# Top-k attention and two MLPs: the softmax division moved from each head to each tile of tokens, with a new order

## The chip, the cores and the metric

One core of a Trainium2 chip runs the whole program. It has a matrix engine (TensorE, PE in the rows), a vector engine (VectorE, DVE), a scalar engine (ScalarE, ACT), GpSimd (POOL), and a sync engine (SP) whose queue issues the DMAs here. The metric is device microseconds (us) of one execution, the median of several.

## The reference

```python
scores = q @ k.T / 8                                   # 4 batches x 8 heads, 576 x 576, head size 64
kth    = the 32nd largest of each row
attn   = softmax(where(scores >= kth, scores, -1e9))
x      = (attn @ v), heads side by side: 2304 tokens x 512
h      = x @ w_in;  x = (h * sigmoid(1.702 h)) @ w_out           # 512 -> 2048 -> 512
h      = x @ w_in2; out = (P(h) / (Q(h) + 1e-6)) @ w_out2        # P cubic, Q = 1 + |b0||h| + |b1|h^2
```

## The kernel before

The 2304 tokens are 18 tiles of 128 rows. Attention runs as 144 steps, one for a tile and a head (tile-major, so eight steps make a tile). A step (`attend`) multiplies q and k on TensorE into a PSUM tile `S`; four rounds of `max` on VectorE, with `match_replace` between them, find the 32nd largest value of each row (tiles `mx`, `E`); ScalarE and GpSimd turn the scores into the numerators of the softmax (`nm`, `E`), split them into a high and a low f16 half (`A`), and a transposing DMA brings them to `AT`. Then `attend_av` makes the second product on TensorE, 15 matmuls into a PSUM slot `misc`, 64 columns of it the head's output and one more the sum of the numerators, because `V` has a column of ones.

Before the change VectorE takes the reciprocal of that sum (`r`, L704), and ScalarE copies the 64 columns from PSUM into the tile's row buffer `x` with `r` as its scale (L705). When a tile's eight heads are there, `x_done` rescales `x` where a group of tiles spans two batches (L756, 6 tiles of 18), makes the f16 high half on ScalarE (L757) and the low half on GpSimd (L758), and a transposing DMA writes `xh` (L760), the input of the first MLP.

The MLPs run in units over groups of two tiles (one in the last two groups): `u_h` (first product, L815), `u_act` (L835 and on), `u_o` (second product, L896 for the first MLP, L893 for the second). The weights of both are prepared on the chip at the start (`w_load`: a conversion on VectorE, L418 and L421, squares and sums on ScalarE, small matmuls L323).

Nobody writes the order of instructions by hand. Each operation is recorded with an engine, a duration, what it reads and writes, and a due time; some name a second engine (`alt`). `Program.schedule` then picks, again and again, the operation that can start first, and among several the one with the smallest due time plus an entry of the table `OFF` (by kind, engine and phase). All engines take their instructions in the order that comes out of this, so an instruction that waits holds up all behind it on its engine. The due times follow from constants such as `LAV` (how many steps the second product lags), `UW` (steps for a unit), `W1P` and `W2P` (when the weights are prepared).

Of the kernel before, what the change touches and what calls it, by code (L numbers as in the profile page):

```python
# [7 lines left out]
F32 = mybir.dt.float32  # L8
# [3 lines left out]
AF = mybir.ActivationFunctionType  # L12
# [209 lines left out]
def kernel(  # L222
# [461 lines left out]
    def attend_av(i, prio):  # L684
# [62 lines left out]
    def x_done(t, prio):  # L747
# [314 lines left out]
LAV = 2.171  # L1062
# [11 lines left out]
KLAG = 7.3553  # L1074
QLAG = 3.6483
NKH = 1
NQH = 1
W1P = -0.5495
W2P = 6.1579
W1R = 0.6406  # L1080
W2R = 0.8231
LATE = 2
MLAG = 3.9112
SWITCH = 59.94
OLAG = 1.2959
UW = 1.2171
ALATE = -329.15
OFF = {
    ('attend', 'ACT'): 4.75,
    ('attend', 'ACT', 0): 0.44,  # L1090
    ('attend', 'ACT', 1): -0.72,
    ('attend', 'ACT', 2): 0.58,
    ('attend', 'ACT', 3): 46.78,
    ('attend', 'ALT'): 22.03,
    ('attend', 'DVE'): 39.57,
    ('attend', 'DVE', 0): 20.59,
    ('attend', 'DVE', 1): -3.17,
    ('attend', 'DVE', 2): -6.61,
    ('attend', 'DVE', 3): 0.24,
    ('attend', 'PE'): -148.65,  # L1100
    ('attend', 'PE', 0): -18.34,
    ('attend', 'PE', 1): 2.41,
    ('attend', 'PE', 2): -17.08,
    ('attend', 'PE', 3): 5.2,
    ('attend', 'POOL'): -5.3,
    ('attend', 'POOL', 0): -19.7,
    ('attend', 'POOL', 1): -32.31,
    ('attend', 'POOL', 2): 7.63,
    ('attend', 'POOL', 3): 3.96,
    ('attend', 'SP'): -25.93,  # L1110
    ('attend', 'SP', 0): -10.33,
    ('attend', 'SP', 1): -14.06,
    ('attend', 'SP', 2): -2.97,
    ('attend', 'SP', 3): 15.67,
    ('attend_av', 'ACT'): -139.96,
    ('attend_av', 'ACT', 0): -44.41,
    ('attend_av', 'ACT', 1): -1.02,
    ('attend_av', 'ACT', 2): 7.97,
    ('attend_av', 'ACT', 3): 6.06,
    ('attend_av', 'ALT'): 2.68,  # L1120
    ('attend_av', 'DVE'): -8.3,
    ('attend_av', 'DVE', 0): 4.69,
    ('attend_av', 'DVE', 1): -6.19,
    ('attend_av', 'DVE', 2): -3.12,
    ('attend_av', 'DVE', 3): 0.88,
    ('attend_av', 'PE'): -70.15,
    ('attend_av', 'PE', 1): 5.75,
    ('attend_av', 'PE', 2): 14.49,
    ('k_prep', 'ACT'): -1.49,
    ('k_prep', 'ACT', 0): 0.39,  # L1130
    ('k_prep', 'ACT', 1): -7.7,
    ('k_prep', 'ACT', 2): 41.38,
    ('k_prep', 'ACT', 3): -6.15,
    ('k_prep', 'ALT'): 7.45,
    ('k_prep', 'DVE'): 27.22,
    ('k_prep', 'DVE', 0): 9.09,
    ('k_prep', 'DVE', 1): -9.7,
    ('k_prep', 'DVE', 2): 51.8,
    ('k_prep', 'DVE', 3): -32.69,
    ('k_prep', 'PE'): 24.7,  # L1140
# [290 lines left out]
```

## Time and profile before

| | us |
|---|---|
| median of 3 runs (1252.35 to 1254.08) | 1253.32 |
| the profiled execution, its own time | 1253.18 |
| its span, from the first to the last instruction | 1251.4 |
| TensorE matmuls busy | 1047.7 (84%) |
| VectorE busy | 1078.1 (86%) |
| ScalarE busy | 1048.0 (84%) |
| GpSimd busy | 773.6 (62%) |

The profiled execution lies 0.14 us under the median, and 1.8 us of its time are outside the span. Busy times overlap, and each is a mean over stages with different limits; a group's busy time counts overlapped stretches of one engine only once, so instructions that follow each other closely add less than their own duration.

### The profile page before, as it was taken

To read this page: it belongs to the slowest core of one execution; us is meant where nothing else is said; L and a number is where in the kernel's file an instruction comes from. 1 tells how busy PE (TensorE), PEld (TensorE's weight loads), DVE (VectorE), ACT (ScalarE), POOL (GpSimd) and SP (SyncE) were. 2 spreads that over 40 slices of the span, in tenths; PEclk is the share of its full clock that TensorE was granted. 3 is DMA by queue.
4 is the path that set the end of the run, shared out by engine and by line. 5 is a ranking of instruction groups with operands and counts; after the bars stand their busy time and mean duration, and the time that the engine had idled before them with its cause. 6 is when DMAs were issued, how large, how long until landed. Compare 5 with 4: busy or idle time off the path is not lost.

```text
span 1251.4 us, 26010 instructions
## 1 busy us (share of the span) xinstructions
PE 1047.7 (84%) x9196; PEld 712.6 (57%) x9196; DVE 1078.1 (86%) x2423; ACT 1048.0 (84%) x1931; POOL 773.6 (62%) x1095
## 2 busy tenths in 40 slices
PE   0223464659899999999999999999999999999998
PEld 0122342537556766676567666756666677676664
DVE  6899999999999999999999999989999997424243
ACT  7989887878989999999998988788888988666675
POOL 6888888876767678766785685467657653211110
PEclk9999995778999999999999999999999999999999
DMA  9847999967889568967697579557856854634375
GB/s 317 251 113 205 204 272 278 266 143 176 174 208 230 92 133 208 220 130 158 154 217 146 113 193 206 116 135 178 188 102 132 214 123 96 194 102 161 118 260 186
DMA packets 366146, 222.44 MB, mean 178 GB/s; under 512 B 316608, under 2 KB 328896, under 8 KB 366016
## 3 DMA queue, kind: packets, MB, share of 16 engines
q1 hardware_dynamic: 366016, 220.78, 71.6%
q8 instruction: 72, 1.18, 0.4%
q14 instruction: 58, 0.48, 0.1%
HBM read 136.32 MB, written 13.11 MB: 119 GB/s over the span
## 4 chain that ended last, share of the span: by engine, by line
PE 37%; DVE 30%; ACT 11%; POOL 8%; DMA 8%; issue 5%; SPq 1%; POOLq 0%; DVEq 0%; ACTq 0%
PE h L815 16%; DVE mx L663 11%; DVE E L665 10%; PE acc L893 9%; PE acc L896 7%; DMA AT<-A 4%; ACT t L835 3%; PE misc L694 3%; PE S L655 2%; POOL A L675 2%; POOL t L839 2%; DVE t L843 1%; DMA ring<-in_moe_w_out_dram 1%; DVE t L848 1%; DVE t L840 1%
## 5 line engine op out<-in xcount | busy, mean ns | idle before, releaser
L663 DVE MAX8 mx<-E 128x8 f32<-128x576 f32 x432 | 319.5, 750 | 2.6
L893 PE MATMUL acc<-ring,t 128*128 128x512 f32 x576 | 270.3, 603 | 7.4 <-DVE t L840 5.3
L675 POOL TENSOR_TENSOR A<-E,A 128x576 f16<-128x576 f32 x144 | 188.4, 1310 | 63.8 <-ACT A L673 58.3
L815 PE MATMUL h<-xh,W 128*128 128x128 f16 (+1 forms) x2688 | 214.1, 240 | 10.8 <-DVE t L848 9.5
L815 PEld LDWEIGHTS <-W 128*128 128x128 f16 x2688 | 193.3, 101 | 38.9 <-issue 14.6
L665 DVE MATCH_REPLACE8 E<-mx,E 128x576 f32<-128x576 f32 x288 | 213.4, 742 | 0.0
L815 PE MATMUL h<-yh,ring 128*128 128x256 f16 (+1 forms) x1920 | 208.8, 263 | 4.3 <-ACT t L835 3.6
L815 PEld LDWEIGHTS <-ring 128*128 128x128 f16 x1920 | 170.6, 98 | 51.6 <-issue 29.5
L839 POOL TENSOR_TENSOR t<-t,t 128x512 f32<-128x512 f32 x114 | 151.9, 1333 | 44.9 <-ACT t L835 35.0
L896 PE MATMUL acc<-W,gh 128*128 128x512 f16 x576 | 173.7, 383 | 0.1
L893 PEld LDWEIGHTS acc<-ring,t 128*128 128x128 f32 x576 | 102.0, 191 | 102.7 <-issue 84.0
L872 POOL TENSOR_TENSOR gl<-t,gh 128x512 f16<-128x512 f32 x72 | 84.4, 1172 | 118.9 <-ACT gh L870 117.7
L655 PE MATMUL S<-K,qs 128*128 128x288 f16 (+1 forms) x640 | 113.8, 308 | 49.9 <-ACT E L668 47.2
L671 ACT ACTIVATE E<-E,nm,ei 128x576 f32<-128x576 f32 x144 | 124.4, 865 | 17.2 <-POOL nm L670 15.9
L835 ACT ACTIVATE t<-h,cf 128x512 f32<-128x512 f32 (+1 forms) x160 | 94.2, 641 | 42.7 <-PE h L815 40.5
L694 PE MATMUL misc<-V,AT 128*128 128x65 f16 (+5 forms) x2400 | 102.9, 200 | 31.6 <-DMA AT<-A 24.5
L694 PEld LDWEIGHTS <-AT 128*128 128x128 f16 (+2 forms) x2400 | 94.1, 104 | 58.9 <-DMA AT<-A 39.0
L668 ACT ACTIVATE E<-S,mx 128x576 f32<-128x576 f32 x144 | 105.7, 736 | 16.8 <-DVE mx L663 10.5
L655 PEld LDWEIGHTS <-qs 128*128 128x128 f16 (+1 forms) x640 | 65.2, 106 | 91.1 <-issue 70.4
L663 DVE MAX8 mx<-S 128x8 f32<-128x576 f32 x144 | 108.3, 754 | 5.2 <-PE S L655 4.2
L896 PE MATMUL acc<-W,gl 128*128 128x512 f16 x288 | 110.2, 382 | 1.9 <-POOL gl L872 1.8
L835 ACT ACTIVATE t<-h,cf,cf 128x512 f32<-128x512 f32 (+1 forms) x160 | 110.5, 745 | 0.0
(161 smaller groups left out, 1807.0 us busy)
## 6 DMA issues: line engine op xcount, KB each, us to landing
ring<-scr SPq DMA_DIRECT2D x160, 512.0 KB, 4.5
ring<-in_moe_w_out_dram SPq DMA_DIRECT2D x12, 1024.0 KB, 7.5
ring<-in_moe_w_in_dram SPq DMA_DIRECT2D x9, 1024.0 KB, 6.8
ld<-in_v_dram SPq DMA_DIRECT2D x32, 256.0 KB, 3.8
out_dram<-t SPq DMA_DIRECT2D x18, 256.0 KB, 4.2
ld<-in_k_dram SPq DMA_DIRECT2D x16, 256.0 KB, 4.2
lq<-in_q_dram SPq DMA_DIRECT2D x32, 128.0 KB, 3.4
yh<-in_moe_w_in_dram SPq DMA_DIRECT2D x4, 1024.0 KB, 8.4
```

The costliest lines, as they stand in the source:

```text
L655: PE.matmul(s[:n, c, :SH], qs[:, 2 * (h % 4) + x, :n], K[:, h % 2, c * SH:(c + 1) * SH], start=(x == 0), stop=(x == 1))
L663: op("DVE", dve(S, not r), lambda r=r: DVE.max(mx[:, r], w.t if r else sv()), [w if r else s], [mx], prio)
L665: op("DVE", dve(S, not r) + 0.068, lambda r=r: DVE.match_replace(w.t if r else two(w.t), mx[:, r], w.t if r else sv(), NEG), [mx, w if r e ...
L668: op("ACT", act(S, True) + APA, lambda: ACT.activation(two(e.t), sv(), AF.Prelu, bias=mx[:, 3, 7:8], scale=-1.0, alpha=NEAR), [s, mx], [e] ...
L671: op("ACT", act(S) + 0.2, lambda: ACT.activation(e.t, e.t, AF.Exp, bias=nm.t, scale=es()), [e, nm, ei], [e], prio)
L675: lo = lambda en: en.tensor_tensor(A[:, 1, :S], e.t, A[:, 0, :S], ALU.subtract)
L694: PE.matmul(ps[r0:r0 + n, :hi - lo], at[:kp, x, j, r0:r0 + n], V[:kp, h % 2, j, lo:hi], start=(j == 0 and lo == D and x == 0), stop=(j == ...
L815: PE.matmul(o, w[:, half, kd * 256 + jj * P: kd * 256 + (jj + 1) * P], xy[:, tl, l * ND + kd, :], start=(kd == 0 and n == 0), stop=(kd == ...
L835: op("ACT", act(w, True) + APA, lambda f2=f2, c=c: ACT.activation(dst[:, c], src[:, c], func, bias=bias(f2) if bias else 0.0, scale=sc(f2) ...
L839: op("POOL", pool_tt(512), lambda: POOL.tensor_tensor(o.t, x.t, y.t, f), [x, y], [o], prio, alt=("DVE", dve(512), lambda: DVE.tensor_tenso ...
L893: PE.matmul(acc[j].t, u.gate[:, c], w[:, jj * DM:(jj + 1) * DM], start=st, stop=sp)
L896: PE.matmul(acc[j].t, l[:, c], w[:, half, jj * DM:(jj + 1) * DM], start=(st and n == 0), stop=(sp and n == 2))
```

## The change

In `attend_av` the reciprocal and the scale go. ScalarE copies all 65 columns, head output and sum, from PSUM into `x`, whose rows now hold 8 heads of 65 numbers. In `x_done` one reciprocal on VectorE takes the tile's eight sums, in 6 tiles a small multiply on VectorE joins the batch factor to them (in place of the ScalarE pass L756), and one multiply over 8 x 64 numbers, due on GpSimd with VectorE as its second engine, normalises the tile. The f16 split then reads `x` with a stride of 65.

```diff
 def attend_av(i, prio):
-            XT[t] = buf("x", [P, DM], F32, NX)
+            XT[t] = buf("x", [P, H, D + 1], F32, NX)
...
-        r = buf("r", [P, 1], F32, 3)
-        op("DVE", TINY, lambda: DVE.reciprocal(r.t, ps[:, D:D + 1]), [ps], [r], prio)
-        op("ACT", act(D, True) + APA, lambda: ACT.activation(x[:, h * D:(h + 1) * D], ps[:, :D], AF.Copy, scale=r.t), [ps, r], [x], prio,
-           alt=("DVE", dve(D, True) + APD, ...
+        op("ACT", act(D + 1, True), lambda: ACT.activation(x[:, h], ps.t, AF.Copy), [ps], [x], prio)
...
 def x_done(t, prio):
+        r = buf("r", [P, H], F32, 2)
+        heads = lambda y: y.rearrange("p (h d) -> p h d", h=H)
+        op("DVE", TINY, lambda: DVE.reciprocal(r.t, x[:, :, D]), [x], [r], prio)
         if t in xrat:
-            op("ACT", act(DM) + APA, lambda: ACT.activation(x.t, x.t, AF.Copy, scale=xrat[t]), [x, gsb[g]], [x], prio)
-        op("ACT", act(DM), lambda: ACT.activation(xs[:, 0], x.t, AF.Copy), [x], [xs], prio, alt=...
-        lo = lambda e: e.tensor_tensor(xs[:, 1], x.t, xs[:, 0], ALU.subtract)
+            op("DVE", TINY, lambda: DVE.tensor_scalar(r.t, r.t, xrat[t], None, ALU.mult), [r, gsb[g]], [r], prio)
+        op("POOL", pool_tt(DM), lambda: POOL.tensor_tensor(x[:, :, :D], x[:, :, :D], r.t.unsqueeze(2).to_broadcast([P, H, D]), ALU.mult), [x, r], [x], prio,
+           alt=("DVE", dve(DM), ...
+        op("ACT", act(DM), lambda: ACT.activation(heads(xs[:, 0]), x[:, :, :D], AF.Copy), [x], [xs], prio, alt=...
+        lo = lambda e: e.tensor_tensor(heads(xs[:, 1]), x[:, :, :D], heads(xs[:, 0]), ALU.subtract)
...
-LAV = 2.171
+LAV = 2.3735
-UW = 1.2171
+UW = 1.2958
...
-    ('attend', 'DVE'): 39.57,
+    ('attend', 'DVE'): 35.7,
...
-RATE = 1.57
-PHASES = (-72.4, 45.3, 173.3)
+RATE = 2.22
+PHASES = (-57.7, 44.4, 205.2)
```

All of `OFF` and the due-time constants have new values, so the scheduler makes a new order on every engine. Counted over the whole program, VectorE loses 144 reciprocals of one column and gets 18 of eight, 6 small multiplies and 5 copies of `acc` to `yc` that ScalarE made before; it gives 3 passes `t<-t,t` to GpSimd. ScalarE keeps 144 copies out of `misc` (65 columns, no scale) and loses the 6 passes of L756. GpSimd gets the 18 multiplies and the 3 passes; all 18 stand on GpSimd.

On VectorE, where the second tile of tokens is in work (S, E and mx belong to heads of the steps 16 and on, ring is weight data, misc holds a finished second product), there stood before:

```order
L418 TENSOR_SCALAR t_1950<-ring 128x512
L418 TENSOR_SCALAR t_1956<-ring 128x512
L704 RECIPROCAL r_1975<-misc 128x1
L663 MAX mx_1888<-E_1916 128x8
L665 MATCH_REPLACE E_1928<-mx_1920,E_1928 128x576
L421 SCALAR_TENSOR_TENSOR ring<-ring,t_1950 128x512
L421 SCALAR_TENSOR_TENSOR ring<-ring,t_1956 128x512
L704 RECIPROCAL r_1985<-misc 128x1
L665 MATCH_REPLACE E_1916<-mx_1888,E_1916 128x576
```

and now, where that tile ends:

```order
L665 MATCH_REPLACE E_1983<-mx_1953,E_1983 128x576
L313 TENSOR_SCALAR qi_2010<-qi_2010 128x1
L663 MAX mx_2057<-S_2012 128x8
L754 RECIPROCAL r_2059<-x_1368 128x8
L315 TENSOR_SCALAR qi_2010<-qi_2010 128x1
L663 MAX mx_1953<-E_1983 128x8
L665 MATCH_REPLACE E_2066<-mx_2057,S_2012 128x576
```

Two reciprocals that waited for a second product on TensorE stood between the `max` and `match_replace` of the following heads; one reciprocal for the tile, which waits for ScalarE's last copy into `x`, stands there now.

On GpSimd, at the end of the same tile, there stood before (xs is the f16 split of x, nm a head's softmax bias, A its low half, yc and ring weight data):

```order
L675 TENSOR_TENSOR A_101<-E_1928,A_101 128x576
L427 TENSOR_TENSOR ring<-ring 128x1024
L316 TENSOR_SCALAR qi_2033<-qi_2033 128x1
L316 TENSOR_SCALAR vsc<-vsc 128x1
L758 TENSOR_TENSOR xs_2087<-x_1314,xs_2087 128x512
L452 TENSOR_TENSOR yc<-ring,yc 128x1024
L669 TENSOR_SCALAR nm_2130<-mx_2013,ei_1095 128x1
```

and now:

```order
L670 TENSOR_SCALAR nm_1999<-nm_1999 128x1
L427 TENSOR_TENSOR yh<-yh 128x1024
L757 TENSOR_TENSOR x_1368<-x_1368,r_2059 128x8x64
L316 TENSOR_SCALAR qi_2010<-qi_2010 128x1
L675 TENSOR_TENSOR A_101<-E_1898,A_101 128x576
L761 TENSOR_TENSOR xs_2077<-x_1368,xs_2077 128x512
L317 TENSOR_SCALAR qi_2010<-qi_2010 128x1
L669 TENSOR_SCALAR nm_2099<-mx_1953,ei_1237 128x1
```

The multiply of the tile stands ahead of a head's low half and of the next head's bias, which wait behind it on GpSimd.

## Rows read from the trace of the kernel before

**Rows 1.** The page, first part: busy us (share of the span) and instructions of each engine.

```profile
PE 1047.7 (84%) x9196; PEld 712.6 (57%) x9196; DVE 1078.1 (86%) x2423; ACT 1048.0 (84%) x1931; POOL 773.6 (62%) x1095
```

**Rows 2.** Busy time by stretch (us from the start), then granted TensorE clock, DMA share, GB/s.

```profile
0.00:150.00 150.00, 40.02 (x279) 29.50 (x279) 129.28 (x339) 127.92 (x225) 121.74 (x179) 1.00 0.79 214
150.00:300.00 150.00, 92.95 (x939) 67.61 (x940) 145.65 (x357) 120.04 (x214) 115.03 (x148) 0.75 0.89 236
300.00:450.00 150.00, 138.93 (x1465) 95.41 (x1462) 146.26 (x336) 136.68 (x278) 104.53 (x166) 0.99 0.79 170
450.00:1055.00 605.00, 585.82 (x5092) 397.24 (x5093) 582.23 (x1274) 535.17 (x981) 407.35 (x577) 1.00 0.71 160
1055.00:1251.40 196.40, 189.96 (x1426) 122.84 (x1423) 74.64 (x121) 128.22 (x237) 24.99 (x29) 0.99 0.51 167
```

**Rows 3.** TensorE's waits from 0 to 300: us in total, times, longest.

```profile
PE misc L323 <- DVE p L322: 89.8, 26, 9.2
PE S L655 <- ACT E L668: 40.4, 15, 7.9
```

**Rows 4.** TensorE's waits from 450 to 1055.

```profile
PE misc L694 <- DMA AT<-A: 5.5, 7, 1.5
PE S L655 <- ACT E L668: 4.1, 6, 1.6
```

**Rows 5.** Line 704, 0 to 300: instructions (ns min/median/max); VectorE's idle time before them.

```profile
L704 DVE RECIPROCAL r<-misc x27: 140/158/169, 81.3 to 288.4; 128x1 f32<-128x1 f32 x27
...
  PE misc L694: 2.7, 5
  ACT x L705: 1.4, 1
  PE misc L323: 0.3, 1
```

**Rows 6.** Line 704, 300 to 450 and 450 to 1055: the same.

```profile
L704 DVE RECIPROCAL r<-misc x25: 139/153/169, 302.7 to 449.7; 128x1 f32<-128x1 f32 x25
...
  PE misc L694: 2.4, 4
...
L704 DVE RECIPROCAL r<-misc x91: 136/155/170, 453.5 to 1053.8; 128x1 f32<-128x1 f32 x91
```

**Rows 7.** VectorE in order of time: start us, duration us.

```profile
601.25 0.14 DVE L704 RECIPROCAL r<-misc 128x1 f32<-128x1 f32 x1
601.37 0.09 DVE L665 MATCH_VALUE_LOAD E<-mx,S 128x8 f32 x1
...
621.66 0.14 DVE L704 RECIPROCAL r<-misc 128x1 f32<-128x1 f32 x1
621.73 0.07 DVE L665 MATCH_VALUE_LOAD E<-mx,E 128x8 f32 x1
```

**Rows 8.** Groups by line: busy us, mean ns, idle us before (with what ended it).

```profile
L704 DVE RECIPROCAL r<-misc 128x1 f32<-128x1 f32 x144 | 22.1, 156 | 15.6 <-PE misc L694 11.8 <-ACT x L705 1.7 <-ACT E L668 0.8
L909 ACT ACTIVATE yc<-acc 128x512 f32<-128x512 f32 x18 | 10.6, 596 | 0.0
```

**Rows 9.** Groups by line, GpSimd's passes over 512 and 1024 columns.

```profile
L839 POOL TENSOR_TENSOR t<-t,t 128x512 f32<-128x512 f32 x114 | 151.9, 1333 | 44.9 <-ACT t L835 35.0 <-DVE t L840 4.1 <-ACT t L862 1.6
L758 POOL TENSOR_TENSOR xs<-x,xs 128x512 f16<-128x512 f32 x18 | 20.9, 1161 | 16.2 <-ACT xs L757 16.2
L452 POOL TENSOR_TENSOR W<-ring,W 128x1024 f16<-128x1024 f32 x5 | 10.9, 2186 | 2.4 <-ACT ring L450 2.4
```

**Rows 10.** Groups by line: ScalarE with a column as its scale and without.

```profile
L705 ACT ACTIVATE x<-misc,r 128x64 f32<-128x64 f32 x144 | 44.4, 309 | 32.1 <-DVE r L704 23.6 <-PE misc L694 3.8 <-DVE t L418 1.5
L756 ACT ACTIVATE x<-x,gr 128x512 f32<-128x512 f32 x6 | 4.3, 718 | 0.0
L757 ACT ACTIVATE xs<-x 128x512 f16<-128x512 f32 x18 | 11.2, 624 | 0.1
```

**Rows 11.** VectorE with two inputs from SBUF: ns min/median/max, and the group's mean.

```profile
L843 DVE SCALAR_TENSOR_TENSOR t<-t,ab,t x72: 727/750/1799, 323.5 to 1238.4; 128x512 f32<-128x512 f32 x72
...
L843 DVE SCALAR_TENSOR_TENSOR t<-t,ab,t 128x512 f32<-128x512 f32 x72 | 63.9, 887 | 52.2 <-ACT t L835 52.2
```

**Rows 12.** Line 760, the DMA of a tile to xh: who waited for it, 0 to 300.

```profile
  PE h L815: 0.9, 1
```

**Rows 13.** The chain that ended last, in order of time: start us, us, what.

```profile
1115.60 2.59 PE acc L896 x12
...
1154.90 2.62 PE h L815 x24
```

More of the change, by code (lines that the diff above doesn't have):

```diff
@@ L702, in attend_av @@
             op("PE", 0.465, lambda r0=r0, n=n, V=V: av(r0, n, V), [at] + [VS[b2, h // 2] for _, _, b2, _ in sg], [ps] + ([x] if h == 0 else []), prio)
-        r = buf("r", [P, 1], F32, 3)
-        op("DVE", TINY, lambda: DVE.reciprocal(r.t, ps[:, D:D + 1]), [ps], [r], prio)
-        op("ACT", act(D, True) + APA, lambda: ACT.activation(x[:, h * D:(h + 1) * D], ps[:, :D], AF.Copy, scale=r.t), [ps, r], [x], prio,
-           alt=("DVE", dve(D, True) + APD, lambda: DVE.tensor_scalar(x[:, h * D:(h + 1) * D], ps[:, :D], r.t, None, ALU.mult)))
+        op("ACT", act(D + 1, True), lambda: ACT.activation(x[:, h], ps.t, AF.Copy), [ps], [x], prio)
     grans, t = [], 0
@@ L754, in x_done @@
         xs = buf("xs", [P, 2, DM], F16, NXS)
+        r = buf("r", [P, H], F32, 2)
+        heads = lambda y: y.rearrange("p (h d) -> p h d", h=H)
+        op("DVE", TINY, lambda: DVE.reciprocal(r.t, x[:, :, D]), [x], [r], prio)
         if t in xrat:
-            op("ACT", act(DM) + APA, lambda: ACT.activation(x.t, x.t, AF.Copy, scale=xrat[t]), [x, gsb[g]], [x], prio)
-        op("ACT", act(DM), lambda: ACT.activation(xs[:, 0], x.t, AF.Copy), [x], [xs], prio, alt=("DVE", dve(DM, x=2), lambda: DVE.tensor_copy(xs[:, 0], x.t)))
-        lo = lambda e: e.tensor_tensor(xs[:, 1], x.t, xs[:, 0], ALU.subtract)
+            op("DVE", TINY, lambda: DVE.tensor_scalar(r.t, r.t, xrat[t], None, ALU.mult), [r, gsb[g]], [r], prio)
+        op("POOL", pool_tt(DM), lambda: POOL.tensor_tensor(x[:, :, :D], x[:, :, :D], r.t.unsqueeze(2).to_broadcast([P, H, D]), ALU.mult), [x, r], [x], prio,
+           alt=("DVE", dve(DM), lambda: DVE.tensor_tensor(x[:, :, :D], x[:, :, :D], r.t.unsqueeze(2).to_broadcast([P, H, D]), ALU.mult)))
+        op("ACT", act(DM), lambda: ACT.activation(heads(xs[:, 0]), x[:, :, :D], AF.Copy), [x], [xs], prio,
+           alt=("DVE", dve(DM, x=2), lambda: DVE.tensor_copy(heads(xs[:, 0]), x[:, :, :D])))
+        lo = lambda e: e.tensor_tensor(heads(xs[:, 1]), x[:, :, :D], heads(xs[:, 0]), ALU.subtract)
         op("POOL", pool_lo(DM), lambda: lo(POOL), [x, xs], [xs], prio, alt=("DVE", dve(DM), lambda: lo(DVE)))
@@ L1073 @@
 VLO = 0
[L1074 to L1075 removed]
+KLAG = 7.0048
+QLAG = 1.5828
 NKH = 1
 NQH = 1
[L1078 to L1081, printed above, removed]
+W1P = -0.2394
+W2P = 6.4044
+W1R = 0.5736
+W2R = 0.8205
 LATE = 2
[L1083 to L1389 removed]
```

548 lines of the change are left out of this document (299 added, 249 removed).

## The prediction

> **What bounds the kernel now.** I read the page's busy times first [rows 1]. VectorE (1078.1), TensorE (1047.7) and ScalarE (1048.0) lie within 3% of each other, so the sums alone name no bound. The split by stretch does [rows 2]. From 0 to 300 us TensorE is busy 133 of 300 (40.0 + 93.0) and VectorE 275 (129.3 + 145.7): TensorE waits, VectorE works. The granted clock of TensorE is 0.75 of full there from 150 to 300, a mix of its two levels (1.2 and 2.4 GHz), with the engine idle for a third of the stretch; since it waits for others, that clock sets little. From 300 to 450 TensorE is busy 138.9 of 150, from 450 to 1055 585.8 of 605, and from 1055 to the end 190.0 of 196.4. So of its 203.7 idle us (1251.4 − 1047.7) 167 lie in the first 300, 11 in the next 150, 19 in the next 605 and 6.4 at the end. From about 300 on the kernel runs at the pace of TensorE; before that at the pace of what feeds it.
>
> The waits of the first 300 us say what feeds it [rows 3]: 89.8 us for `p`, VectorE's last step before the small matmuls of the scales, and 40.4 us for the step that frees a score tile, which follows four rounds of `max`. Both are VectorE's queue. From 450 to 1055 the two waits for the attention chain are 5.5 and 4.1 us in all [rows 4].
>
> The reader is to take this from it: a microsecond taken from VectorE's queue ahead of 300 us moves the start of the full stretch, and the work behind it is as long as before. The same microsecond taken later lets VectorE finish earlier while TensorE has the same work left.
>
> **The change part by part.**
>
> *VectorE's queue, 0 to 300.* 27 reciprocals stand there [rows 5]. One lasts 156 ns [rows 8], but the next instruction starts 0.12 or 0.07 us after it [rows 7]; I take 0.10. That is 27 × 0.10 = 2.7 us (bounds 27 × 0.07 = 1.9 and 27 × 0.156 = 4.2). VectorE also stood idle ahead of them, 2.7 + 1.4 + 0.3 = 4.4 us in 7 waits [rows 5], since a reciprocal waits for a second product and everything behind it waits too. In their place come one reciprocal a tile, three in this stretch: 3 × 0.10 = 0.3 us for the instructions, and waits for ScalarE's last copy, which the trace of before can't show. Bounds: nothing, or the 1.4 us of its one wait for such a copy, three times (4.2); I take the mean of the 7 waits, 4.4 / 7 = 0.63, three times, 1.9. Sum: −2.7 − 4.4 + 0.3 + 1.9 = −4.9 us.
>
> *The same, 300 to 450.* 25 reciprocals (2.5 us) and 2.4 us of idle time [rows 6], less three tile reciprocals with their waits (2.2) and two of the new small multiplies (0.2): −2.5 us of VectorE's queue. TensorE still idles for 11 of 150 us, so some of it counts; I take −1.5 (bounds 0 and −2.5).
>
> *The same, 450 to 1055.* 91 reciprocals [rows 6] at 0.10 are 9 us off VectorE, but TensorE idles for 19 of 605 us, and only 9.6 of them are waits for the attention chain [rows 4]. I take −1 (bounds 0 and −9.6).
>
> *ScalarE.* 144 scaled copies of 64 columns become plain ones of 65. The price of a scale from a column is the difference of two passes over 512 columns, 718 − 624 = 94 ns [rows 10], so 144 × 0.094 = 13.5 us go; the six passes of L756 (4.3) and five of the 18 `yc` copies (5 × 0.6 = 3.0 [rows 8]) go too, and so do the 23.6 us that ScalarE stood idle for a reciprocal [rows 10], in exchange for waits for TensorE directly. ScalarE is behind VectorE in the first 300 us (248 busy against 275 [rows 2]), so I book nothing for it (bounds 0 and, for the 27 early copies, −2.5).
>
> *VectorE's new work.* Five `yc` copies, one of them in the early stretch: at ScalarE's 0.6 us [rows 8], +0.6 (bounds 0 and +0.6).
>
> *GpSimd.* 18 multiplies over 512 columns. The nearest row has the same shape and type: 1.33 us [rows 9]; the broadcast second input and the stride of 65 are in no row, so the bounds are 1.16 (the f16 pass of 512) and 2.19 (the pass of 1024). Three stand ahead of 300 us, six ahead of 450. They are hidden where GpSimd has room: it is busy 121.7 + 115.0 of 300 us [rows 2]. They also lengthen a tile's way to the MLP, by a reciprocal, the multiply and their handing over, some 1.7 us. TensorE's waits for that DMA are 0.9 us in all in this stretch [rows 12], so there is cover, and if it is gone one tile in three shows its 1.7: +1.0 (bounds 0 and 3 × 2.19 + 0.5 = 7.1).
>
> *Two engines at one memory.* VectorE's passes with two inputs from SBUF have a median of 750 ns, a mean of 887 and a maximum of 1799 [rows 11]: now and then one waits about a microsecond for something. On the 72 of this line that is 72 × 0.137 = 9.9 us. If it scales with GpSimd's busy time, which grows by 24 us to 798 (3%), the line gets 0.3 us more, and all such lines perhaps three times that. I take +0.4 for the early stretch (bounds 0 and 6 × 1.05 = 6.3, if each of the six early multiplies holds a pass up by 1799 − 750 ns).
> The Trainium skill ("SBUF — State Buffer", Who interferes with whom) says that VectorE and GpSimd share one port pair, that a VectorE instruction with two SBUF inputs and a GpSimd instruction that reads SBUF exclude each other, and that the second to come is blocked for the whole instruction. By that rule a multiply of 1.3 us on GpSimd may cost VectorE up to as much again, while `max` and `match_replace`, with one input each, go free.
>
> *The order.* It is new everywhere, but the places are near the old ones: by the count of TensorE's queue, 1,176 matmuls of first products stood ahead of the 55th second product, and 1,200 now; 1,080 of them stood behind the last second product and 1,128 now, and 105 of L896 in place of 96. 48 and 9 are 2 × 2.62 + 9 × 2.59 / 12 = 7.2 us [rows 13]: so much of TensorE's work has moved from before the last head to after it. Its total is the same, so I book nothing for the order itself; but the last head has to be ready 7.2 us earlier for the same end, and 7.2 + 5.4 = 12.6 us for my forecast. VectorE's queue gives 143 × 0.10 = 14.3 us up to there and the idle time of its reciprocals, so this is just within reach.
>
> Sum: −4.9 − 1.5 − 1.0 + 0.6 + 1.0 + 0.4 = −5.4 us, on 1253.2 of the profiled execution, which is 0.14 under the median: **1247.8 us**.
>
> **The rivals.** A difference under 0.2% (2.5 us) is about what a measurement of this kernel can't tell from no change.
>
> *VectorE counts all the way* (chance 0.12). If attention sets the pace until 1055, all of it counts: 22.1 us of reciprocals less 18 × 0.156 = 2.8 and the six small multiplies (0.9) is 18.4, and 1253.2 − 18.4 = 1235. For it: VectorE is busy 96% from 450 to 1055 [rows 2]. Against it: TensorE is busy 97% there, and what it waits for attention is 9.6 us.
> The Trainium skill ("Perfetto Trace Analysis", Identifying the Most-Contended Engine) says to look for the engine with the highest occupancy, and not to trust matmul busy time but weight-load busy time for TensorE. By that rule TensorE stands at 57% and VectorE at 86% over the span, and the whole 18.4 us would come back. After 1055 the rows go against it: VectorE is busy 75 of 196 us and TensorE 190.
>
> *It is hidden anyway* (0.16). The early waits are for `p` and the scales of the weights, which hang on DMAs and GpSimd as well, and the waits of the tile reciprocals (up to 4.2 us) eat the gain. Then −2.7 − 4.4 + 0.3 + 4.2 = −2.6, +2.0 for the three additions: 1252.6.
>
> *GpSimd's queue takes it back, and more* (0.19). In the first 450 us GpSimd is busy 341 of 450 and its queue is in order; the order shows the multiply ahead of a head's low half and of the next head's bias. If each of the six early multiplies delays its head by its whole length, at 1.33 us that is 8.0 in place of my 1.0, and the time is 1254.8; at 2.19 us it is 13.1, and the time 1259.9. It turns to slower from 1.5 us a multiply on the path (6 × 1.5 = 9.0 against 1.0 + 5.4 + 2.5 = 8.9).
>
> **How the numbers follow.** My forecast, the early stretch of VectorE, has 0.53, with a range of its own from 1243 to 1250.5. The first rival gives 1235, the second 1252.6, the third 1255 to 1260. A range from 1238 to 1257 leaves out most of the first and half of the third, about 2 in 10. Faster by over 0.2%: 0.53 + 0.12 = 0.65; within: 0.16; slower: 0.19.
>
> **What would show it.** In the profile after: VectorE 15 to 20 us less busy; no reciprocal that waits for a second product; L703 on ScalarE near 0.22 us; the multiply near 1.3 us; TensorE's busy time up to 300 us a few us higher and its idle sum near 198 in place of 203.7; the stretch after the last second product about 7 us longer. I am wrong if TensorE's idle time before 300 us is not smaller, if the multiply is far over 1.3 us, or if TensorE's idle time from 450 to 1055 changes by more than a few us, for then the order, not the reciprocals, moved the time.

## The result, and the profile after

| | before | changed |
|---|---|---|
| median of 6 runs each, us | 1253.7 (1252.35 to 1256.89) | 1262.64 (1259.24 to 1266.03) |
| ratio, 95% interval | | 1.0063 [1.0042, 1.0084] |
| profiled execution, its span | 1251.4 | 1261.8 |

The change made the kernel 0.6% slower: above the forecast (1247.8) and above the top of its range (1257).

The page's busy times of the changed kernel, to set beside [rows 1]:

```profile
PE 1043.2 (83%) x9196; PEld 714.6 (57%) x9196; DVE 1070.6 (85%) x2305; ACT 1029.4 (82%) x1920; POOL 807.7 (64%) x1116
```

VectorE lost 7.4 us of busy time and ScalarE 18.6, TensorE 4.5; GpSimd gained 34.1, and the span grew by 10.4. So the time went into waits. The split by stretch, against [rows 2]; the columns are busy us of TensorE, its weight loads, VectorE, ScalarE and GpSimd, then the granted clock, the DMA share and GB/s:

```profile
0.00:150.00 150.00, 33.84 (x216) 24.79 (x217) 128.38 (x325) 125.30 (x218) 124.11 (x174) 1.00 0.78 219
150.00:300.00 150.00, 90.30 (x976) 68.79 (x975) 144.16 (x338) 114.62 (x209) 120.03 (x150) 0.81 0.84 214
300.00:450.00 150.00, 140.04 (x1462) 97.27 (x1463) 141.96 (x314) 136.20 (x287) 110.07 (x177) 0.99 0.85 186
450.00:1055.00 605.00, 578.73 (x5036) 393.77 (x5035) 578.68 (x1204) 517.23 (x961) 425.51 (x587) 1.00 0.70 158
1055.00:1261.80 206.80, 200.31 (x1510) 129.95 (x1507) 77.45 (x128) 136.09 (x248) 27.98 (x31) 0.99 0.51 163
```

TensorE was busy 8.8 us less by 300 us (124.1 against 133.0) and 7.1 us less from 450 to 1055; 10.4 us more of its work is left behind 1055 (1510 matmuls against 1426). The 8.8 us are not all work left undone. By 300 us 1192 matmuls had run against 1218, and the granted clock from 150 to 300 was 0.81 against 0.75: the same matmul of `W` and `gh` has a mean of 379 ns there in place of 417. Its waits from 0 to 300, and from 450 to 1055, against [rows 3, 4] (us in total, times, longest):

```profile
PE misc L323 <- DVE p L322: 95.8, 24, 9.8
PE S L655 <- ACT E L668: 34.6, 14, 5.5
...
PE S L655 <- DMA K<-kh: 8.1, 2, 7.5
PE h L818 <- DMA xh<-xs: 7.5, 1, 7.5
```
```profile
PE misc L694 <- DMA AT<-A: 9.6, 9, 2.0
PE S L655 <- ACT E L668: 8.8, 13, 1.7
```

New in the first list are two long single waits, 7.5 us for a head's keys and 7.5 us for `xh`, the first tile that comes to the MLP. The first is no delay: the product that waits for the keys starts at 82.6 us, and at 83.4 in before. The second is one. The groups of the new operations (busy us, mean ns, idle us ahead of them):

```profile
L757 POOL TENSOR_TENSOR x<-x,r 128x512 f32<-128x512 f32 x18 | 19.8, 1097 | 8.7 <-DVE r L754 6.1 <-DVE qi L313 0.9 <-PE acc L899 0.6
L703 ACT ACTIVATE x<-misc 128x65 f32<-128x65 f32 x144 | 31.5, 220 | 19.4 <-PE misc L694 16.4 <-PE misc L323 2.0 <-DVE c L312 0.4
L754 DVE RECIPROCAL r<-x 128x8 f32<-128x8 f32 x18 | 3.5, 194 | 2.5 <-ACT x L703 2.5
L756 DVE TENSOR_SCALAR r<-r,gr 128x8 f32<-128x8 f32 x6 | 2.7, 447 | 0.0
```

The two costly ones are as cheap as forecast or cheaper (multiply 1.10 us for 1.33, copy 0.22). The small ones are dearer: 0.19 us for a reciprocal of eight, and 0.45 for each of the six small multiplies, for which the prediction had 0.1 to 0.15. The rows so far accuse the order, and do not prove it.

### The profile page after: what moved, and what is told of

Same layout as the page of the kernel before. It is cut to its first block, busy times and chain, and to the rows that moved or that the text cites. A ratio compares the mean times of both kernels' runs of the same rounds, so it can differ in the third digit from the quotient of the medians.

```text
span 1261.8 us, 25932 instructions
## 1 busy us (share of the span) xinstructions
PE 1043.2 (83%) x9196; PEld 714.6 (57%) x9196; DVE 1070.6 (85%) x2305; ACT 1029.4 (82%) x1920; POOL 807.7 (64%) x1116
## 4 chain that ended last, share of the span: by engine, by line
PE 36%; DVE 29%; ACT 12%; POOL 8%; DMA 7%; issue 5%; SPq 0%; DVEq 0%; POOLq 0%; ACTq 0%
PE h L818 15%; DVE mx L663 11%; PE acc L896 10%; DVE E L665 10%; PE acc L899 6%; DMA AT<-A 4%; PE misc L694 3%; ACT t L838 3%; PE S L655 2%; POOL t L842 2%; DVE t L846 1%; DMA lq<-in_q_dram 1%; POOL A L675 1%; ACT E L668 1%; DVE t L851 1%
## 5 line engine op out<-in xcount | busy, mean ns | idle before, releaser
L818 PEld LDWEIGHTS <-W 128*128 128x128 f16 x2688 | 194.5, 101 | 46.9 <-issue 23.6
L818 PE MATMUL h<-yh,ring 128*128 128x256 f16 (+1 forms) x1920 | 205.2, 262 | 3.8 <-ACT t L838 3.7
L842 POOL TENSOR_TENSOR t<-t,t 128x512 f32<-128x512 f32 x117 | 155.0, 1326 | 46.8 <-ACT t L838 32.8
L671 ACT ACTIVATE E<-E,nm,ei 128x576 f32<-128x576 f32 x144 | 124.5, 867 | 26.3 <-POOL nm L670 25.1
L694 PE MATMUL misc<-V,AT 128*128 128x65 f16 (+5 forms) x2400 | 103.1, 200 | 28.2 <-DMA AT<-A 19.2
L663 DVE MAX8 mx<-S 128x8 f32<-128x576 f32 x144 | 108.4, 753 | 12.5 <-PE S L655 12.2
L846 DVE SCALAR_TENSOR_TENSOR t<-t,ab,t 128x512 f32<-128x512 f32 x72 | 59.5, 826 | 62.8 <-ACT t L838 62.5
```

The source lines that it names most:

```text
L663: op("DVE", dve(S, not r), lambda r=r: DVE.max(mx[:, r], w.t if r else sv()), [w if r else s], [mx], prio)
L671: op("ACT", act(S) + 0.2, lambda: ACT.activation(e.t, e.t, AF.Exp, bias=nm.t, scale=es()), [e, nm, ei], [e], prio)
L694: PE.matmul(ps[r0:r0 + n, :hi - lo], at[:kp, x, j, r0:r0 + n], V[:kp, h % 2, j, lo:hi], start=(j == 0 and lo == D and x == 0), stop=(j == ...
L818: PE.matmul(o, w[:, half, kd * 256 + jj * P: kd * 256 + (jj + 1) * P], xy[:, tl, l * ND + kd, :], start=(kd == 0 and n == 0), stop=(kd == ...
L842: op("POOL", pool_tt(512), lambda: POOL.tensor_tensor(o.t, x.t, y.t, f), [x, y], [o], prio, alt=("DVE", dve(512), lambda: DVE.tensor_tenso ...
```

## The experiments

Most kernels below are built so that every engine's sequence is that of before or of the changed kernel, or a piece of each. The two in the next section, and those made from the first of them, put other operations into the places of a given schedule. The kernels named h_, e1_late_tile0 and after_t0_forward record all operations of the changed kernel, and a written list (PLAN) hands them out in place of the scheduler. "The order" takes in which engine an operation with two possible engines goes to. A ratio is against the kernel before on the same chip; two ratios that differ by 0.003 or less are hardly apart.

```diff
-    order = pr.schedule(SWITCH)
+    order = pr.replay(PLAN)
```

### Operations and order apart

*e1_newops_oldorder*: the new operations at the places of the old ones.

```diff
-        op("DVE", TINY, lambda: DVE.reciprocal(r.t, ps[:, D:D + 1]), [ps], [r], prio)
+        op("DVE", TINY, lambda: None, [ps], [r], prio)
...
+            copy(x[:, h], ps.t)
+            if done_heads[t] == H and t not in xrat:
+                normalise(t, x)
```

> The changed operations (no per-head reciprocal, plain copy of 65 columns, one reciprocal of eight and one multiply on GpSimd per tile) set into the order of the kernel before: every engine's sequence is that of before, less the removed instructions and with the new ones where a tile's last copy stands. Theory O (the new order lost the time, the operations alone gain a little): 1248 to 1252 us, ratio 0.995 to 0.999. Theory W (the added work, above all the 18 multiplies in GpSimd's queue and the longer way from a tile's last head to its f16 split, lost it): 1258 to 1264, ratio 1.004 to 1.008.

1255.27 us, ratio 0.9995 [0.9977, 1.0013], between the ranges of the two theories.

*e2_oldops_neworder*: the other half, the old operations in the new order.

```diff
-        op("ACT", act(D + 1, True), lambda: ACT.activation(x[:, h], ps.t, AF.Copy), [ps], [x], prio)
+            DVE.reciprocal(r1.t, ps[:, D:D + 1])
+            ACT.activation(x[:, h * D:(h + 1) * D], ps[:, :D], AF.Copy, scale=r1.t)
```

> The reverse: the operations of before (a reciprocal and a scaled copy per head, the batch factor as a ScalarE pass) set into the order of the changed kernel, each at the place of that kernel's copy. Theory O: as slow as the changed kernel or a few us slower, 1262 to 1270, ratio 1.006 to 1.013. Theory W: near the kernel before, 1252 to 1256, ratio 0.999 to 1.002.

1277.14 us, 1.0188 [1.0147, 1.0229], slower than both theories had it. The two halves do not add up to the whole. In this kernel ScalarE waits 63.4 us for reciprocals, against 23.6 in before [rows 10], since each stands at the place of a copy in an order that was not made for it:

```profile
L708 ACT ACTIVATE x<-misc,r 128x64 f32<-128x64 f32 x144 | 44.9, 312 | 68.9 <-DVE r L707 63.4 <-DVE qi L313 2.7 <-DVE qi L312 0.8
```

So what the order costs depends on the operations in it: 0.0188 with the old ones, and 0.0068 or 8.5 us with the new ones (1.0063 less 0.9995). The change ships the new ones, and all that follows is about these 8.5 us. In before's order the new operations neither gain nor lose. Two questions follow: where the order loses, and why operations that were forecast to save 5 us save nothing.

### Which part of the order loses

Four kernels with the new operations take one order up to the end of the 34th head (some 300 us) or of the 101st (770 us) and the other from there on. Their only edit is the content of PLAN.

*h_old34_new*:

> The changed operations; the order of before up to the end of the 34th head's step (some 300 us), then the new order for all that is left. Theory E (the new order loses its time early, where TensorE waits for the first tiles): 1253 to 1257 us. Theory L (it loses it late, with 7.2 us more of TensorE's work behind the last head, or in the middle): 1260 to 1265.

*h_new34_old*:

> The changed operations; the new order up to the end of the 34th head's step, then the order of before for the rest. Theory E: 1260 to 1265 us. Theory L: 1253 to 1257.

*h_old101_new*:

> The changed operations; the order of before up to the end of the 101st head's step (some 770 us), then the new one. Theory E: 1253 to 1257 us. Theory L, if the place is the work behind the last head: 1260 to 1265; if it is the middle: 1253 to 1257.

*h_new101_old*:

> The changed operations; the new order up to the end of the 101st head's step, then the order of before. Theory E: 1260 to 1265 us. Theory L, last head: 1253 to 1257; middle: 1260 to 1265.

Measured: 1.0035 [1.0013, 1.0058], 1.0063 [1.0042, 1.0084], 0.9984 [0.9963, 1.0005], 1.0075 [1.0049, 1.0102]. With the new order in the first 34 heads alone all of the loss is there, as theory E had it; with the new order behind the 101st head alone nothing is lost. But h_old34_new, 0.0040 over e1_newops_oldorder and between the ranges of both theories, loses some 5 us with before's order in the first 34 heads. So the early order is enough for the loss, and the first 34 heads are not the only place where time can be lost.

In the early order the first tile comes late. Its transfer to `xh`, and the first matmul of the MLP, in before, in the changed kernel and in e1_newops_oldorder (start us, duration), with a score product beside it in the last two:

```profile
135.96 1.29 SPq L760 DMA_TRANSPOSE xh<-xs  x1
142.35 5.03 PE L815 MATMUL h<-xh,W 128*128 128x128 f16 x48
```
```profile
147.69 1.47 SPq L763 DMA_TRANSPOSE xh<-xs  x1
154.36 1.44 PE L818 MATMUL h<-xh,W 128*128 128x128 f16 x12 [7.45 <-DMA xh<-xs]
159.12 1.12 PE L655 MATMUL S<-K,qs 128*128 128x288 f16 x4 [3.32 <-ACT E L668]
```
```profile
138.16 1.23 SPq L780 DMA_TRANSPOSE xh<-xs  x1
141.10 1.12 PE L655 MATMUL S<-K,qs 128*128 128x288 f16 x4
...
143.14 4.07 PE L835 MATMUL h<-xh,W 128*128 128x128 f16 x48
```

The last second product of that tile starts at 131.5 us in before, 131.9 in e1 and 137.3 in the changed kernel; from there to the transfer it is 4.5, 6.3 and 10.4 us. So of the 11.7 us by which the transfer is late, 5.8 are heads that end later (the cause of that is open), 1.8 the new operations (as in e1), and 4.2 queues, GpSimd's above all: from the multiply to the low half it is 5.5 us, and 1.8 in e1. GpSimd in order of time in the changed kernel shows the queue:

```profile
141.09 1.38 POOL L757 TENSOR_TENSOR x<-x,r 128x512 f32<-128x512 f32 x1
...
142.98 2.38 POOL L452 TENSOR_TENSOR yc<-yh,yc 128x1024 f16<-128x1024 f32 x1
...
146.55 1.12 POOL L761 TENSOR_TENSOR xs<-x,xs 128x512 f16<-128x512 f32 x1
```

Between the tile's multiply and its low half stands a pass over weights.

Is the late tile the loss, or a sign of it? *h_old_t0_new* and *h_new_t0_old* cut the two orders at this transfer (PLAN again):

> The new operations, in the order of before until the first tile's transfer to the MLP is issued (the close of the 8th head, some 138 us in), and in the new order from there on. With before's order to the end of the 34th head the ratio was 1.0035 and with the new order all the way 1.0063. Theory F (what the new order loses is the 10 us by which it brings the first tile to the MLP later): the loss is gone, 1252 to 1256 us, ratio 0.999 to 1.002, and the first tile's transfer starts near 138 us. Theory S (the order from the first tile to the 34th head carries the loss, and the late first tile is only a sign of it): 1259 to 1265 us, ratio 1.004 to 1.009.

> The reverse: the new operations, in the new order until the first tile's transfer is issued, then in the order of before. With the new order to the end of the 34th head the ratio was 1.0063. Theory F (the first tile's lateness is the loss): 1260 to 1266 us, ratio 1.005 to 1.010, the first tile's transfer at 146 to 149 us. Theory S (the loss lies between the first tile and the 34th head): 1252 to 1257 us, ratio 0.999 to 1.003, though the first tile comes just as late.

*e1_late_tile0* leaves before's order and moves only the close of the first tile (85 places of PLAN, with the next head's second product now ahead of the first MLP matmul):

```diff
-['x_done', 0]:1 to :5    at places 676 to 689 of PLAN
+['x_done', 0]:1 to :5    85 places later
```

> The new operations in the order of before, with one thing moved: the five closing steps of the first tile (its reciprocal, multiply, two halves and the transfer) stand about 10 us later in the queues, and its first MLP products behind the second products of the next head. Nothing else moves. Theory F (a first tile that comes late costs its lateness, since TensorE has no other work there): the transfer starts 7 to 11 us later than the 138 us of the same operations in before's order, and the time is 1261 to 1265 us, ratio 1.005 to 1.009. Rival (the late first tile costs nothing by itself, TensorE catches up later; the loss is in what VectorE and TensorE did in place of it ahead of the first tile): 1253 to 1257 us, ratio 0.999 to 1.003.

h_new_t0_old: 1264.3 us, 1.0068 [1.0045, 1.0091], as theory F had it. h_old_t0_new: 1267.51, 1.0095 [1.0069, 1.0121], where F had no loss, and above the range of S too. e1_late_tile0: 1269.42, 1.0114 [1.0089, 1.0140]. In the last one the tile was 18 us later than in e1, more than meant:

```profile
155.96 1.34 SPq L810 DMA_TRANSPOSE xh<-xs  x1
161.46 5.28 PE L865 MATMUL h<-xh,W 128*128 128x128 f16 x48 [8.36 <-DMA xh<-xs]
```

What becomes of a delay is best seen in one number per head: the start of its first `max` (the one that reads `S`), less the same in before. Each is worked out from two traces; the tail is the span less the start of the last one, 1038.71 in before. A trace is one execution, and executions of one kernel differ by some us (h_old101_new: 1250.9 to 1256.7), so only differences well above that count:

| head | e1 | late_tile0 | new_t0_old | old_t0_new | changed | old101_new |
|---|---|---|---|---|---|---|
| 9th | +0.6 | +1.4 | +9.2 | +0.2 | +9.6 | +1.3 |
| 17th | -0.6 | +14.2 | +9.6 | +3.9 | +1.8 | +1.5 |
| 33rd | +1.1 | +13.5 | +8.4 | +13.3 | +9.6 | +0.8 |
| 73rd | +1.0 | +17.0 | +9.7 | +17.0 | +13.3 | +1.7 |
| 144th | +1.6 | +16.3 | +12.4 | +8.2 | +5.1 | -1.8 |
| tail (before: 212.7) | 213.4 | 213.4 | 213.4 | 217.9 | 218.0 | 217.9 |

A delay from ahead of 150 us is carried to the last head nearly whole: TensorE, busy 707.9 of 740.3 us from 300 us to the last head in e1, has little spare time in which to catch up. In the two kernels with before's order behind the first tile, h_new_t0_old and e1_late_tile0, the first MLP matmul comes 12.5 and 18.3 us later than in e1, and that costs 9.2 and 14.9 us (ratios less 0.9995, times 1254), 0.7 to 0.8 us for each us. In the first of them the next head is late too (+9.2 at the 9th); in the second only the tile is (+1.4). That shows that a late first tile is enough for the loss. It does not show that it is all of it: in h_old_t0_new the transfer is on time (137.83 us), and the loss is there all the same. TensorE's queue shows where its first matmul of the MLP stands:

```profile
148.87 1.12 PE L702 MATMUL S<-K,qs 128*128 128x288 f16 x4 [7.16 <-ACT E L715]
149.79 1.49 PE L865 MATMUL h<-xh,W 128*128 128x128 f16 x12
161.21 1.12 PE L702 MATMUL S<-K,qs 128*128 128x288 f16 x4 [9.94 <-ACT E L715]
```

A head's score product stands ahead of the MLP there, and another one behind its 12th matmul; each waits for a free score tile (7.2 and 9.9 us), and the MLP waits behind them. In e1 a score product stands ahead of the MLP too, but it starts at 141.10 us without a wait, and the first 48 matmuls of the MLP follow each other. The changed kernel has the same cut behind the 12th matmul; the product there waits 3.3 us. In h_old_t0_new 13 us are lost by the 33rd head. The order from the first tile to the 34th head is a second way to lose as much, in a kernel with a seam at that point; the two do not add up (1.0063 with both). How they share the loss in the changed kernel stays open.

One more try, *after_t0_forward*, moved the steps of the first tile forward within the new order:

```diff
-['attend', 0 to 7], ['attend_av', 0 to 7], ['x_done', 0]    where the new order has them
+the same                                                     up to 45 places of PLAN earlier
```

> The changed kernel in its new order, with one thing moved: the steps of the first tile (its 8 heads and its close) go forward in the queues by up to 45 places of the order, ramped from 63 us on, so that its transfer stands where before had it (some 138 us); other steps around it fall back by as much. Theory F (the first tile's lateness is the loss): the transfer starts at 137 to 141 us, the last head's max ends 7 to 10 us earlier than the 1043.8 us of the new order, the tail behind it stays at 218 us, and the time is 1252 to 1256 us, ratio 0.998 to 1.002. Rival (it is the whole early order, not this tile): 1259 to 1265 us, ratio 1.004 to 1.009.

1282.86 us, 1.0206 [1.0180, 1.0233], a miss for both theories. The transfer came later, not sooner, and VectorE was busy 110.7 of the first 150 us in place of 128.4:

```profile
158.08 3.24 SPq L810 DMA_TRANSPOSE xh<-xs  x1
```

That fits steps which stand ahead of others in a queue before their inputs are there, and hold up the rest; no run shows it. This run shows nothing on the cause.

### What a reciprocal costs, and VectorE's time

In order of time on VectorE, e1 (second) has no reciprocal where before (first) has one [rows 7]:

```profile
600.58 0.75 DVE L663 MAX8 mx<-S 128x8 f32<-128x576 f32 x1
601.25 0.14 DVE L704 RECIPROCAL r<-misc 128x1 f32<-128x1 f32 x1
601.37 0.09 DVE L665 MATCH_VALUE_LOAD E<-mx,S 128x8 f32 x1
```
```profile
601.51 0.75 DVE L663 MAX8 mx<-S 128x8 f32<-128x576 f32 x1
602.30 0.09 DVE L665 MATCH_VALUE_LOAD E<-mx,S 128x8 f32 x1
```

From the `max` to the load it is 0.79 us in both, with a reciprocal between them or without. The load needs the result of the `max`; instructions that need nothing of it start about 0.66 us after it, as the reciprocals in the rows of five below do. So this reciprocal filled a gap. Two runs put unread reciprocals back into e1, at the old places:

```diff
-        op("DVE", TINY, lambda: None, [ps], [r], prio)
+            for _ in range(k):                       # e1_recip1: 1, e1_recip5: 5
+                DVE.reciprocal(r.t, ps[:, D:D + 1])
```

> The new operations in the order of before, and where before had its reciprocal of a head's sum, five unread reciprocals of that sum on VectorE (720 in all, 135 in the first 300 us). Prediction's price of 0.07 to 0.10 us each: VectorE's queue gets 9 to 13 us longer ahead of 300 us and 50 to 72 us in all; if a us of VectorE ahead of 300 us moves the start, the time rises by at least 9 us, ratio 1.007 or more. Gap theory (one short independent instruction fits between two dependent passes for nothing, the other four cost 0.07 each): 27 x 4 x 0.07 = 7.5 us ahead of 300 us, ratio 1.005 to 1.008, and the pitch from the pass before to the pass behind the five is about 0.79 + 4 x 0.07 = 1.07 us in the trace. Rival (VectorE is not what the early stretch waits for): ratio 0.999 to 1.003, TensorE's busy time to 300 us as with the same order without them (134.0 us).

> The new operations in the order of before, with one unread reciprocal of each head's sum on VectorE, in the place where before had its reciprocal (144 in all). Gap theory (a reciprocal fits into the 0.12 us that a pass that depends on the one before has to wait anyway): as without them, 1253 to 1257 us, ratio 0.999 to 1.002. The prediction's price (0.10 us and its wait, some 4.9 us ahead of 300 us): ratio 1.003 to 1.007.

Five: 1370.03 us, 1.0907 [1.0875, 1.0938]. One: 1263.52 us, 1.0059 [1.0037, 1.0082]. Gap theory and the prediction's price both had the five too cheap by far, since five that write one column follow each other at 0.2 us:

```profile
599.65 0.74 DVE L663 MAX8 mx<-E 128x8 f32<-128x576 f32 x1
600.31 0.96 DVE L708 RECIPROCAL rr<-misc 128x1 f32<-128x1 f32 x5
601.19 0.07 DVE L665 MATCH_VALUE_LOAD E<-mx,S 128x8 f32 x1
```

From the `max` to the load it is 1.54 us, 0.75 over the 0.79, times 144 = 108 us, for a loss of 115. Work added to VectorE counts in full here. And one reciprocal a head is not free: 0.0064 over e1, 8 us, against the gap theory; its ratio lies in the 1.003 to 1.007 that the prediction's price gave. *e1_recip1_nowait* splits that price:

```diff
-                DVE.reciprocal(r.t, ps[:, D:D + 1])
+                DVE.reciprocal(r.t, c1)
```

> e1_recip1 with the unread reciprocal reading a constant, so that it takes its time on VectorE (144 x 0.07 to 0.156) and waits for nothing. If the price of 8 us is the instruction's time: 1260 to 1265 us, ratio 1.004 to 1.008. If it is the wait for a second product in front of VectorE's queue (5.4 us of it stood behind 300 us in e1_recip1): 1253 to 1258 us, ratio 0.998 to 1.002.

1258.48 us, 1.0029 [1.0011, 1.0047]: between the two and between the ranges of both theories: about half the instruction's time (4 us, 0.03 us each) and half the wait for a second product, each half at the edge of what two ratios tell apart.

Does work taken from VectorE count as well? Two kernels leave out a pass of the search for the 32nd value:

```diff
-                op("DVE", ..., lambda r=r: DVE.match_replace(...
+                op("DVE", ..., (lambda: None) if r == 2 and i < 34 else lambda r=r: DVE.match_replace(...
```

(`i >= 34` in e1_short_late).

> The new operations in the order of before, with the third match_replace left out in the first 34 heads, 34 x 0.74 us or, from pass to pass, up to 0.79: some 21 us less for VectorE ahead of 300 us (27 heads), 25 us in all; it leaves out a part of the top-k, so the output is another one. The prediction's premise (a us taken from VectorE ahead of 300 us moves the start of the full stretch): 10 to 21 us less, 1233 to 1245 us, ratio 0.983 to 0.993. Rival (the early stretch waits for a row of other engines and transfers besides; VectorE's shorter passes only give it idle time): 1250 to 1255 us, ratio 0.997 to 1.001.

> The same with the third match_replace left out in the heads behind the 34th: 110 x 0.74 to 0.79 = 81 to 87 us less for VectorE, all of it behind 300 us; a part of the top-k is left out. The prediction's premise (from 300 us on the pace is TensorE's): TensorE's idle time from 300 us to the last head's max is 740.3 - 707.9 = 32.4 us in the same order with all passes, and its waits for the attention chain a third of it, so 3 to 12 us less, ratio 0.990 to 0.998. Rival (VectorE sets the pace all the way to the last head, as the 115 us for five reciprocals a head say): the gain goes as far as TensorE lets it, 25 to 32 us, ratio 0.974 to 0.981, with TensorE busy 99% from 300 us to the last head.

e1_short_early: 1255.38 us, 1.0004 [0.9989, 1.0020]. e1_short_late: 1249.15 us, 0.9936 [0.9912, 0.9960]. By stretch, e1 first, then short_early:

```profile
0.00:150.00 150.00, 39.06 (x275) 28.54 (x276) 129.82 (x330) 126.72 (x224) 122.31 (x180) 1.00 0.79 213
150.00:300.00 150.00, 94.95 (x929) 68.12 (x926) 146.21 (x339) 118.06 (x214) 117.79 (x149) 0.73 0.88 232
```
```profile
0.00:150.00 150.00, 39.83 (x279) 29.25 (x279) 125.64 (x310) 125.90 (x224) 123.90 (x180) 1.00 0.77 213
150.00:300.00 150.00, 92.76 (x949) 67.53 (x948) 136.13 (x301) 119.05 (x216) 120.30 (x150) 0.76 0.88 235
```

VectorE is 14.3 us less busy by 300 us, and TensorE hardly gains: 132.6 us busy against 134.0, with 1227 matmuls against 1200 at a slightly higher clock. The time that came free on VectorE went into its own waits, 38.2 us idle in place of 24.0. It waits for TensorE's score products (2.5 us in e1) and for ScalarE's sums of squares L437, the inputs of `p` (10.2 us in three rows, 5.5 in e1), of which one row each:

```profile
DVE mx L663 <- PE S L655: 6.0, 7, 2.9
DVE p L322 <- ACT yh L437: 4.4, 4, 2.7
```

And from 300 to the last head's `max`, short_late:

```profile
300.00:1030.00 730.00, 705.28 (x6385) 480.78 (x6383) 640.98 (x1278) 639.30 (x1227) 515.47 (x747) 1.00 0.74 166
```

VectorE is busy 88% there and TensorE 97%, and 81 us off VectorE (110 passes of 0.74) gave 7.4 (0.9936 against 0.9995; the profiled execution is 6 us faster than the median). That fits a pace that is TensorE's.

### What the closing steps cost

If a reciprocal a head costs 5 to 8 us, taking them away must have been paid back. Three kernels leave out a tile's closing steps, the last the multiply alone; their copies take a constant factor, and the output is left unnormalised:

```diff
 def normalise(t, x):
-        DVE.reciprocal(r.t, x[:, :, D])
...
-        POOL.tensor_tensor(x[:, :, :D], x[:, :, :D], r.t.unsqueeze(2).to_broadcast([P, H, D]), ALU.mult)
+        return
```

> The new operations in the order of before, without a tile's closing steps: neither the reciprocal of 8 sums (18) nor the six small multiplies on VectorE nor the multiply on GpSimd (18); the copies take a constant factor of 2^-14 so that the halves stay in range, and the output is left unnormalised. Adding up (the closing steps cost 7 to 8 us in before's order, as much as the reciprocals gave): 1246 to 1249 us, ratio 0.992 to 0.995. Saturation (with TensorE as near the bound as VectorE, less work on VectorE or GpSimd gives nothing): 1253 to 1257 us, ratio 0.998 to 1.001.

> The same without the closing steps (the output is left unnormalised), and with the 144 unread reciprocals of e1_recip1. That kernel with the closing steps stood at 1.0059. Either theory: back to 1252 to 1257 us, ratio 0.997 to 1.001, since these are the operations of before but for the factor of the copies and six passes on ScalarE. If it stays at 1.004 or more, the closing steps are not what the time went to, and the copies that no longer wait for the reciprocal are left.

> The new operations in the order of before without the multiply on GpSimd; the tile's reciprocal and the small multiplies stay on VectorE, unread; the copies take a constant factor of 2^-14, and the output is left unnormalised. Without all closing steps the ratio was 0.9952, with all 0.9995. If the multiply in GpSimd's queue is the price: 1248 to 1251 us, ratio 0.994 to 0.997. If the reciprocal with its wait on VectorE is the price: 1253 to 1256 us, ratio 0.998 to 1.001.

| in before's order | with closing steps | without multiply | without closing steps |
|---|---|---|---|
| no reciprocals per head | 0.9995 | 0.9964 [0.9949, 0.9979] | 0.9952 [0.9932, 0.9971] |
| 144 reciprocals | 1.0059 | | 0.9990 [0.9974, 1.0005] |

Down a column the reciprocals cost 4.8 us (without closing steps) and 8.0 (with them); along a row the closing steps cost 5.4 and 8.7. Within what the ratios tell apart they add up, and in before's order they cancel. Of the 5.4 the multiply is some 3.9 (0.9995 - 0.9964, with intervals that just overlap), the rest 1.5, which the intervals do not tell from nothing.

No version here beats both kernels beyond doubt: the best that computes everything, h_old101_new, has 0.9984 with an interval that reaches 1.0005.

## Why the prediction was wrong

**The order, booked at nothing: +8.5 us.** This is the step that failed and put the time outside the range. "Its total is the same, so I book nothing for the order itself" counted TensorE's work, and not when its inputs come. I looked at where the work behind the last head stands, which moved by 7.2 us of matmuls, and not at the first tile, which comes 11.7 us late, nor at the score products that wait ahead of and between its matmuls on TensorE. That a late tile is enough is shown, and that the order behind it is enough in h_old_t0_new; how they share the 8.5 us is not. In spans against e1: the last head 3.6 us later (1043.85 against 1040.30) and the tail 4.5 us longer, 8.1 together. The work moved behind the last head fits both the longer tail and the heads' making up for some of the delay (+13.3 at the 73rd head, +5.1 at the last); by itself it costs nothing that the ratio shows, as in h_old101_new (last head 3.3 us earlier than in e1, tail 4.5 longer). The prediction's own signs of error came true: TensorE's idle time before 300 us is not smaller (175.9 us for 167.0), and from 450 to 1055 it went from 19.2 to 26.3 us. VectorE is 7.4 us less busy where 15 to 20 were forecast.

**"A microsecond taken from VectorE's queue ahead of 300 us moves the start".** Refuted: 25 us off VectorE in the first 34 heads (34 passes of 0.74) gave nothing (1.0004). VectorE's being busy 275 of 300 and last in most of TensorE's waits did not make it the limit; the wait for `p` ends with VectorE's small step, but with shorter work ahead of it that step waits longer for ScalarE's sums. e1_short_early still waits 88.3 us for `p` (90.6 in e1):

```profile
PE misc L323 <- DVE p L322: 88.3, 26, 9.3
```

What sets the early pace instead was not settled. The Trainium skill ("Perfetto Trace Analysis", Identifying the Most-Contended Engine) would have VectorE as the engine to relieve, by its occupancy; against it stand these 25 us for nothing and the 81 for 7.4.

**The reciprocals.** They did give something, 4.8 to 8.0 us where my terms, before the tile reciprocals, had 7.1 ahead of 300 us and 4.9 from there to 450, of which the sum took 1.5 net. The size is near, but the place is not: by the traces e1_recip1 lies 0.4 us behind e1 at the 33rd head and 7.1 at the last, so the gain comes behind 300 us (one trace each; the pair without closing steps shows 1.1 at the last head). I had priced 450 to 1055 at 1.0, with a bound of 9.6, the waits for the attention chain [rows 4]. The bound was the better guide, and about 7 us is also all that e1_short_late got.

**The multiply on GpSimd.** I took 1.0 (bounds 0 and 7.1); it costs some 3.9, or 0.22 us a tile if it is spread over all 18. Its duration was below my row (1.10 for 1.33 us), so its length is not what was wrong. Which tiles pay stays open: by the traces e1_nomult is ahead of e1 by 2.8 us at the 33rd head and 3.3 at the last, but e1_noclose, which lacks the multiply too, is 1.2 behind at the 33rd. The longer way of a tile to the MLP, some 1.7 us by forecast, measured 1.8 on the first tile. That GpSimd's queue takes the gain back was a rival at 0.19: right in part, but its 1255 to 1260 us were to come from six early multiplies at full length.

**The rest.** The tile reciprocals (2.2 forecast for the first three tiles, 1.5 measured for all with the small multiplies, not told from 0) are not contradicted. ScalarE at nothing (e1_recip1_noclose, 0.9990, holds copies with a constant in place of the column scale, and the interval holds 1), the price of the scale (0.094 us forecast, 0.309 - 0.220 = 0.089 measured) and the copies' 0.22 us were right. The +0.4 for two engines at one memory is not to be seen. GpSimd's busy time grew by 34 us where 24 were forecast. The Trainium skill ("SBUF — State Buffer", Who interferes with whom) lets a VectorE pass with two SBUF inputs wait for such a multiply; in the changed kernel, with those 34 us, the passes with two inputs took less than in [rows 11]:

```profile
L846 DVE SCALAR_TENSOR_TENSOR t<-t,ab,t 128x512 f32<-128x512 f32 x72 | 59.5, 826 | 62.8 <-ACT t L838 62.5
```

Together: operations -5 to -8 and +5 to +9, measured -0.6 (0.9995), the order +8.5. The second rival, "It is hidden anyway", also ends at -0.6; it has that number by luck, since its gain was to be eaten by the waits of the tile reciprocals, and not by the multiply.

## What to carry to other kernels

When a change comes with a new order, compare first when each stage's first input arrives (here the first tile at the MLP): here a delay ahead of the full stretch was carried to the end nearly whole, and a saving elsewhere must pay for it. Look also at what waits ahead of and between the first matmuls of that stage in TensorE's queue. With two engines both 96 to 97% busy, work added to the one counted in full here, and of work taken from it little came back. The engine that ends a wait is not yet the one that causes it: shorten its work in a trial run before pricing a gain there.

## What the runs showed of the hardware

A short VectorE instruction that stands between a pass and one that needs its result can be free: 0.79 us from `max` to the dependent load with a reciprocal between them or without, in the rows above. Spread over all 144 places, reciprocals that wait for nothing cost some 0.03 us each (e1_recip1_nowait) for a duration of 0.15. Five that write the same column take 0.2 us each. And 18 GpSimd multiplies with a broadcast second input took 1.07 to 1.10 us in the mean, less than the passes of the same size with two full inputs [rows 9].
